# Packing the matmuls of a score bound into column strips and moving the work around them, in a segmented attention and GLU kernel

## The chip, the cores and the metric

The kernel runs on one core of one Trainium2 chip. The metric is the device time of one execution in microseconds (us), as median of several runs. All runs used below are of the fast state. The engines are PE (tensor engine), PEld (its weight loads), DVE (vector), ACT (scalar), POOL (GpSimd) and SP, whose queue (SPq) issues most of the DMA transfers.

## The reference

Input x has 2048 tokens of 640 features, in bf16. The sequence is cut into four segments of 512 tokens; there are 32 heads of 20 features.

```python
xn = layernorm(x)
q, k, v = xn @ wq, xn @ wk, xn @ wv
for s in range(4):                               # segments
    logits = qs @ ks.T * scale + causal_mask
    a_dot  = softmax(logits) @ vs
    a_mem  = (phi(qs) @ M) / (phi(qs) @ z + 1e-6)
    o      = g * a_mem + (1 - g) * a_dot
    M, z   = M + phi(ks).T @ vs, z + sum(phi(ks))
s   = o @ wo
glu = (sigmoid(xn @ w_gate) * (xn @ w_up)) @ w_down
out = x + s * silu(glu)
```

## The kernel before

Each segment has 20 slots. A slot computes scores of four heads (tile Sps), their exponentials on ACT (pt), the product of earlier exponentials with V (Aps), and takes further PE work from a plan (projections of the next segment, memory update) and from a queue of dense GLU matmuls. The program emits PE's instructions in the order of this plan, so the plan decides which work PE has next.

The softmax is kept in range by a bound on each score: for a head and a query, the sum over the 20 features of |q| times the largest |k| in the segment. It is a small matrix product, with minus the largest |k| as weights, nonzero only at the features of each head (tile ik), and |q| as moving operand (tile aq). The result goes as a 21st row next to the 20 rows of q, against a row of ones in k, so the score matmul subtracts it.

```python
def bound_mm(n, half):                       # twice per segment, 16 heads each
    ik, aq = seg[n]["ik"], seg[n]["aq"]
    cps = ps_d.tile([16, L], F32, name="cps", tag="d")
    for i in range(3):                       # three chunks of 128 features
        nc.tensor.matmul(cps[:], lhsT=ik[:, i, :], rhs=aq[:, i, :], start=(i == 0), stop=(i == 2))
    cb = stg.tile([16, L], BF, name="cb", bufs=2)
    nc.vector.tensor_copy(cb[:], cps[:])
    seg[n]["cb", half] = cb

def bound_dma(n, half, engs):                # SBUF to SBUF, one row per head
    cb = seg[n]["cb", half]
    for r in range(4):
        engs[r % len(engs)].dma_start(QT[32*r + DH:32*r + E1, 4*half:4*half + 4, :], cb[4*r:4*r + 4, :])

def scores(unit):                            # E1 = 21 rows
    ...
    nc.tensor.matmul(Sps[:, r, c0:c0 + ncol], lhsT=KT[32*r:32*r + E1, g, ...],
                     rhs=QT[32*r:32*r + E1, g, q0:L], ..., tile_position=(32*r, 0))

# plan of segment n for the next segment m (slot, work):
for slot, fn, c in [(9, do_K, 0), (10, do_K, 1), (11, do_K, 2), (11, do_Q, 0), (12, do_Q, 1), (13, do_Q, 2),
                    (14, do_Q, 3), (15, do_Q, 4), (16, do_K, 3), (17, do_K, 4)]: ...
for i in range(8): at(10 + i, V_NS, do_V, m, i // 2, i % 2, nc.scalar)
... at(13, 800, m_update, n, 0); at(14, 520, m_update, n, 1)
... at(15, C_NS, bound_mm, m, 0) ... at(19, C_NS, bound_mm, m, 1)

# first segment: three gate/up pairs run before the first scores
do_gate(0, 0); do_up(0, 0); bound_mm(0, 1); ...
for f in (1, 2): do_gate(0, f); do_up(0, f)
```

## Time and profile before

| | before |
|---|---|
| median, first four runs | 343.95 us (343.78 to 344.16) |
| span of the profiled run | 342.0 us |
| PE / DVE / ACT busy | 97% / 65% / 65% |
| share of PE in the chain of waits | 86% |
| bound matmuls | 24, in eight groups of three |

The page of the profiled execution of the kernel before, its first part (busy time of each engine, share of the span, instructions) and the head of its fourth (the chain of work that ended last, by engine):

```profile
span 342.0 us, 8153 instructions
PE 331.2 (97%) x3327; PEld 183.8 (54%) x3370; DVE 221.4 (65%) x516; ACT 221.8 (65%) x218; POOL 100.1 (29%) x172
...
PE 86%; DVE 5%; ACT 4%; issue 3%; POOL 1%; ACTq 0%; POOLq 0%
```

PE is the bottleneck. A matmul's busy time is modelled and overlaps with the next one (0.379 us is shown below where the next starts after 0.218 us), so for sizes it is better to look at when the next instruction starts. The view of the tile cps, and the timeline around one bound group (start us, duration us, engine, line, operation, count), kernel before:

```profile
L287 PE MATMUL cps<-aq,ik x24: 379/379/383, 23.4 to 253.2; 128*16 128x512 bf16 x24
L289 DVE CAST cb<-cps x8: 669/679/679, 25.1 to 253.6; 16x512 bf16<-16x512 f32 x8
```

```profile
91.69 0.81 PE L287 MATMUL cps<-aq,ik 128*16 128x512 bf16 x3
92.35 0.42 ACT L306 CAST V<-psv 128x320 bf16<-128x320 f32 x1
92.44 0.41 PE L467 MATMUL Sps<-QT,KT 21*128 21x384 bf16 x8
```

The three matmuls hold PE from 91.69 to 92.44 us, 0.75 us. In the recorded starts they are 0.218 us apart, and the next kind of matmul starts 0.311 us after the third. Eight groups make 6.0 us. The same timeline at the first scores of the program, and who PE waited for (total us, times, longest us):

```profile
27.95 2.58 SPq L295 DMA_DIRECT2D QT<-cb  x4
...
33.72 0.40 PE L467 MATMUL Sps<-QT,KT 21*128 21x512 bf16 x4
```

```profile
PE up L380 <- ACT tg L374: 0.9, 1, 0.9
PE psv L301 <- DVE ktd L244: 0.8, 1, 0.8
PE Sps L467 <- ACT pt L475: 0.5, 1, 0.5
```

The first scores start without a wait, and the named waits later on are few and below 1 us each.

### The profile page before, as it was taken

The numbers are of one execution on the slowest core, as the hardware profiler recorded it, in microseconds if no ns is written. First come the engines' busy times: TensorE is split into PE (matmuls) and PEld (weight loads), VectorE is DVE, ScalarE is ACT, GpSimd is POOL, SyncE is SP. The second block draws the span as 40 slices with busy tenths as digits, with TensorE's granted clock in tenths as the row PEclk, the third lists the DMA queues.
The fourth block names the chain that finished last, engine by engine and source line by source line (L and its number), as shares of the span: only waits on it lengthen the run. The fifth ranks groups of instructions, "written<-read, shape, count | busy, mean of one in ns | idle before, by whom it ended". The sixth has DMA issues, their size and how long they took to land.

```text
span 342.0 us, 8153 instructions
## 1 busy us (share of the span) xinstructions
PE 331.2 (97%) x3327; PEld 183.8 (54%) x3370; DVE 221.4 (65%) x516; ACT 221.8 (65%) x218; POOL 100.1 (29%) x172
## 2 busy tenths in 40 slices
PE   8999999999999999999999999999999999999995
PEld 3544444656544555556566455545446655544763
DVE  5374465475776776798768786878765575553355
ACT  2523777677786866766787657667965766767620
POOL 6800224223222243223232422222223223232122
PEclk9999999999999999999999999999999999999999
DMA  7987792302247614113365326014134000000132
GB/s 220 384 320 211 156 306 101 80 2 84 86 143 140 154 44 120 49 67 105 80 187 149 79 77 98 21 65 144 36 108 136 22 21 21 20 21 2 58 67 77
DMA packets 51574, 36.45 MB, mean 107 GB/s; under 512 B 27345, under 2 KB 50257, under 8 KB 51537
## 3 DMA queue, kind: packets, MB, share of 16 engines
q1 hardware_dynamic: 50224, 32.00, 33.7%
q10 hardware_dynamic: 1312, 3.93, 2.9%
q8 instruction: 26, 0.43, 0.5%
q14 instruction: 12, 0.09, 0.1%
HBM read 17.05 MB, written 12.32 MB: 86 GB/s over the span
## 4 chain that ended last, share of the span: by engine, by line
PE 86%; DVE 5%; ACT 4%; issue 3%; POOL 1%; ACTq 0%; POOLq 0%
PE yp L394 16%; PE up L380 14%; PE gp L371 13%; PE psq L239 11%; PE Aps L496 9%; PE Sps L467 7%; PE psv L301 6%; PE sp L418 4%; PE am L356 2%; PE cps L287 2%; ACT pt L475 1%; PE dm L337 1%; PE sp L448 1%; ACT mn L317 1%; ACT V L306 1%
## 5 line engine op out<-in xcount | busy, mean ns | idle before, releaser
L475 ACT ACTIVATE pt<-Sps 128x2048 bf16<-128x2048 f32 (+1 forms) x81 | 150.3, 1855 | 35.2 <-PE Sps L467 32.0
L477 POOL TENSOR_SCALAR_AFFINE_SELECT pt<-pt 128x512 bf16<-128x512 bf16 x128 | 80.7, 646 | 226.7 <-ACT pt L475 226.7
L380 PE MATMUL up<-xnT,Wu 128*128 128x512 bf16 x228 | 59.1, 379 | 1.7 <-ACT tg L374 0.9
L371 PE MATMUL gp<-xnT,Wg 128*128 128x512 bf16 x225 | 58.9, 379 | 1.0 <-ACT V L306 0.2
L394 PE MATMUL yp<-Wd,hT 128*128 128x320 bf16 x384 | 57.5, 299 | 0.0
L383 DVE SCALAR_TENSOR_TENSOR hT<-tg,up 128x512 bf16<-128x512 bf16 x48 | 32.8, 684 | 35.9 <-PE up L380 26.6
L496 PEld LDWEIGHTS <-pt 128*128 128x128 bf16 x1280 | 42.7, 96 | 14.4 <-issue 3.0
L374 ACT ACTIVATE tg<-gp 128x512 bf16<-128x512 f32 x48 | 28.5, 594 | 26.0 <-PE gp L371 26.0
L496 PE MATMUL Aps<-V,pt 128*128 128x21 bf16 x1280 | 44.6, 173 | 0.0
L394 PEld LDWEIGHTS <-hT 128*128 128x128 bf16 x384 | 35.3, 97 | 15.3 <-issue 2.6
L398 DVE SCALAR_TENSOR_TENSOR aa<-t,yp 128x320 bf16<-128x320 bf16 x32 | 15.6, 488 | 32.8 <-ACT t L397 32.7
L380 PEld LDWEIGHTS <-Wu 128*128 128x128 bf16 x240 | 21.1, 97 | 24.4 <-issue 4.3
L371 PEld LDWEIGHTS <-Wg 128*128 128x128 bf16 x240 | 21.4, 97 | 23.7 <-issue 3.2
L467 PE MATMUL Sps<-QT,KT 21*128 21x128 bf16 (+3 forms) x512 | 32.3, 301 | 0.5 <-ACT pt L475 0.5
L301 PE MATMUL psv<-Wv,xnT 128*128 128x320 bf16 x160 | 26.5, 299 | 1.1 <-DVE ktd L244 0.8
L397 ACT ACTIVATE t<-yp 128x320 bf16<-128x320 f32 x32 | 13.9, 435 | 20.0 <-PE yp L394 19.7
L239 PE MATMUL psq<-xnT,Wq 128*128 128x512 bf16 x93 | 24.0, 378 | 0.4
L239 PE MATMUL psq<-xnT,Wk 128*128 128x512 bf16 x91 | 23.7, 378 | 0.5
L467 PEld LDWEIGHTS <-KT 21*128 21x128 bf16 x512 | 9.5, 92 | 26.8 <-issue 26.3
L306 ACT CAST V<-psv 128x320 bf16<-128x320 f32 x32 | 13.7, 427 | 15.1 <-PE psv L301 14.7
L301 PEld LDWEIGHTS <-xnT 128*128 128x128 bf16 x160 | 15.4, 98 | 11.4 <-issue 1.1
L418 PE MATMUL sp<-Wo,oT 128*128 128x320 bf16 x120 | 20.2, 298 | 0.2 <-ACT tg L374 0.2
(77 smaller groups left out, 309.1 us busy)
## 6 DMA issues: line engine op xcount, KB each, us to landing
KT<-Kd SPq DMA_DIRECT2D x32, 80.0 KB
QT<-Qd SPq DMA_DIRECT2D x32, 80.0 KB
out_dram<-xt SPq DMA_DIRECT2D x15, 160.0 KB
Wg<-in_B_w_gate_dram ACTq DMA_DIRECT2D x1, 1920.0 KB
Wu<-in_B_w_up_dram ACTq DMA_DIRECT2D x1, 1920.0 KB
xt<-in_A_x_dram SPq DMA_DIRECT2D x3, 640.0 KB
Wd<-in_B_w_down_dram SPq DMA_DIRECT2D x1, 1920.0 KB
Xd<-xn SPq DMA_DIRECT2D x12, 160.0 KB
```

Of the source, the lines that this page charges most:

```text
L239: nc.tensor.matmul(ps[:], lhsT=W[:, k, c * P:(c + 1) * P], rhs=xnT_of[n][:, k, :], start=(k == 0), stop=(k == DC - 1))
L301: nc.tensor.matmul(ps[:], lhsT=xnT_of[n][:, k, j * P:(j + 1) * P], rhs=Wv[:, k, half * HD:(half + 1) * HD], start=(k == 0), stop=(k == DC ...
L371: nc.tensor.matmul(gp[:], lhsT=Wg[:, k, f * P:(f + 1) * P], rhs=xnT_of[n][:, k, :], start=(k == 0), stop=(k == DC - 1))
L374: nc.scalar.activation(tg[:], gp[:], ACT.Tanh, scale=0.5)
L380: nc.tensor.matmul(up[:], lhsT=Wu[:, k, f * P:(f + 1) * P], rhs=xnT_of[n][:, k, :], start=(k == 0), stop=(k == DC - 1))
L383: nc.vector.scalar_tensor_tensor(out=h[:], in0=seg[n]["tg"][:], scalar=1.0, in1=up[:], op0=ALU.add, op1=ALU.mult)
L394: nc.tensor.matmul(yp[:], lhsT=s["hT"][f][:, j * P:(j + 1) * P], rhs=Wd[:, f, hs], start=(f == 0), stop=(f == FC - 1))
L418: nc.tensor.matmul(sp[:], lhsT=s["oT"][:, c, j * P:(j + 1) * P], rhs=Wo[:, c, hs], start=(c == 0), stop=(c == DC - 1))
L467: nc.tensor.matmul(Sps[:, r, c0:c0 + ncol], lhsT=KT[32 * r:32 * r + E1, g, kb * P:(kb + 1) * P], rhs=QT[32 * r:32 * r + E1, g, q0:L], star ...
L475: nc.scalar.activation(pt[:, :, 0:ntot], Sps[:, :, 0:ntot], ACT.Exp, scale=SCALE)
L477: nc.gpsimd.affine_select(out=pt[:, :, c0:c0 + P], in_=pt[:, :, c0:c0 + P], compare_op=ALU.is_ge, fill=0.0, base=0, pattern=[[0, 4], [1, P ...
L496: nc.tensor.matmul(acc["ps"][:, qb, r, :], lhsT=t[:, r, off:off + P], rhs=V[n % 2][:, kb, 4 * g + r, :], start=acc["fresh"], stop=True, sk ...
```

## The change

Its intent is to make the bound cheaper on PE. One group of five matmuls per segment replaces two groups of three. The five go into three strips of 32 columns of the PE array, so that up to three run at once. The three partial sums are not added: they go to the scores as rows 21 to 23, and the score matmul adds them. The bound now passes through DRAM to reach its rows. Since one group needs all of Q and K, these projections are squeezed into slots 9 to 14, and V, phi and the memory update move later. The start is re-ordered too (blocks of x before weights, the first transpose in two parts, index masks built later), and a fourth gate/up pair runs before the first scores. In the excerpt, `...` marks cuts, and lines of the bound functions that only allocate or hand on tiles are left out.

```diff
+    Bd = [dpool.tile([3 * H, L], BF, name=f"Bd{i}") for i in range(2)]
 ...
-    def bound_mm(n, half):
-        cps = ps_d.tile([16, L], F32, name="cps", tag="d")
-        for i in range(3):
-            nc.tensor.matmul(cps[:], lhsT=ik[:, i, :], rhs=aq[:, i, :], start=(i == 0), stop=(i == 2))
+    def bound_mm(n):
+        cps = ps_d.tile([3 * H, L], F32, name="cps", tag="d")
+        for c in range(DC):                                   # DC = 5, H = 32
+            i = c % 3
+            nc.tensor.matmul(cps[H * i:H * i + H, :], lhsT=ik[:, c, :], rhs=aq[:, c, :],
+                             start=(c < 3), stop=(c >= 2), tile_position=(0, H * i), skip_group_check=True)
+        nc.vector.tensor_copy(cb[:], cps[:])
+        nc.sync.dma_start(Bd[n % 2][:], cb[:])
+    def bound_dma(n, half):
+        src = Bd[n % 2][:].rearrange("(i r g) n -> r i g n", i=3, r=4)
+        for r in range(4):
+            nc.sync.dma_start(QT[32*r + DH:32*r + DH + 3, 4*half:4*half + 4, :], src[r][:, 4*half:4*half + 4, :])
 ...
-                                 lhsT=KT[32 * r:32 * r + E1, g, ...
+                                 lhsT=KT[32 * r:32 * r + DH + 3, g, ...
 ...  (the start: cut)
-    for f in (1, 2):
+    for f in (1, 2, 3):
 ...
-(9, do_K, 0), (10, do_K, 1), (11, do_K, 2), (11, do_Q, 0), (12, do_Q, 1), (13, do_Q, 2), (14, do_Q, 3), (15, do_Q, 4), (16, do_K, 3), (17, do_K, 4)
+(9, do_K, 0), (10, do_K, 1), (10, do_K, 2), (11, do_Q, 0), (11, do_Q, 1), (12, do_Q, 2), (12, do_Q, 3), (13, do_Q, 4), (13, do_K, 3), (14, do_K, 4)
-            at(10 + i, V_NS, do_V, m, i // 2, i % 2, nc.scalar)
+            at(12 + i, V_NS, do_V, m, i // 2, i % 2, nc.scalar)
-        at(13, 800, m_update, n, 0)
+        at(17, 800, m_update, n, 0)
-        at(15, C_NS, bound_mm, m, 0)   ...   at(19, C_NS, bound_mm, m, 1)
+        at(16, C_NS, bound_mm, m)
```

More of the change, by code (lines that the diff above doesn't have):

```diff
@@ L134 @@
     beta_b = cpool.tile([P, H], BF, name="beta_b")
-    for half in range(2):
-        load_x(0, ((2 * half, 2 * half + 1), (2 * half + 1, 2 * half + 2)))
-        hs = slice(half * HD, (half + 1) * HD)
-        nc.sync.dma_start(Wv[:, :, hs], A_wv[:, hs].rearrange("(c p) n -> p c n", p=P))
+    for half, blocks in ((0, (0, 1)), (1, (2,)), (None, (3,))):
+        load_x(0, [(j, j + 1) for j in blocks])
+        if half is not None:
+            hs = slice(half * HD, (half + 1) * HD)
+            nc.sync.dma_start(Wv[:, :, hs], A_wv[:, hs].rearrange("(c p) n -> p c n", p=P))
     load_w(nc.sync, Wk, A_wk)
@@ L151 @@
     nc.gpsimd.memset(KT[:].bitcast(mybir.dt.uint32), 0x3F803F80)
-    Ind = []
-    for hb in range(2):
-        t = cpool.tile([P, 3, 4, 4], F32, name=f"Ind{hb}")
-        nc.gpsimd.memset(t[:], -1.0)
-        base = 2 * hb * P - 16 * hb * DH
-        nc.gpsimd.affine_select(out=t[:], in_=t[:], compare_op=ALU.is_ge, fill=0.0, base=base,
-                                pattern=[[P, 3], [-DH, 4], [-4 * DH, 4]], channel_multiplier=1)
-        nc.gpsimd.affine_select(out=t[:], in_=t[:], compare_op=ALU.is_ge, fill=0.0, base=DH - 1 - base,
-                                pattern=[[-P, 3], [DH, 4], [4 * DH, 4]], channel_multiplier=-1)
-        Ind.append(t)
+    Ind = cpool.tile([P, DC, 4, NG], F32, name="Ind")
     V = [cpool.tile([P, 4, H, E1], BF, name=f"V{i}") for i in range(2)]
@@ L167, in late_constants @@
         nc.gpsimd.tensor_copy(BD[:, 0:1], after[:, 0:1])
+        nc.gpsimd.memset(Ind[:], -1.0)
+        nc.gpsimd.affine_select(out=Ind[:], in_=Ind[:], compare_op=ALU.is_ge, fill=0.0, base=0,
+                                pattern=[[P, DC], [-DH, 4], [-4 * DH, NG]], channel_multiplier=1)
+        nc.gpsimd.affine_select(out=Ind[:], in_=Ind[:], compare_op=ALU.is_ge, fill=0.0, base=DH - 1,
+                                pattern=[[-P, DC], [DH, 4], [4 * DH, NG]], channel_multiplier=-1)
         for i in range(2):
@@ L267, in relayout @@
             eng.dma_start(dst[32 * r:32 * r + DH, 4 * half:4 * half + 4, :], src[r])
-    def bound_q(n, half):
-        aq = stg.tile([P, 3, L], BF, name="aq")
-        U16 = mybir.dt.uint16
-        nc.vector.tensor_scalar(aq[:].bitcast(U16), seg[n]["qt"][:, 2 * half:2 * half + 3, :].bitcast(U16),
-                                0x7FFF, None, op0=ALU.bitwise_and)
-        seg[n]["aq"] = aq
-    def bound_k(n, half):
-        ik = stg.tile([P, 3, 16], BF, name="ik", bufs=2)
-        nc.vector.tensor_tensor(
-            ik[:], Ind[half][:].rearrange("p c r g -> p c (r g)"),
-            seg[n]["kabs"][:, 2 * half:2 * half + 3].unsqueeze(2).to_broadcast([P, 3, 16]), op=ALU.mult)
-        seg[n]["ik"] = ik
@@ L283, in bound_mm, with bound @@
-    def bound_mm(n, half):
-        ik, aq = seg[n]["ik"], seg[n]["aq"]
-        cps = ps_d.tile([16, L], F32, name="cps", tag="d")
-        for i in range(3):
-            nc.tensor.matmul(cps[:], lhsT=ik[:, i, :], rhs=aq[:, i, :], start=(i == 0), stop=(i == 2))
-        cb = stg.tile([16, L], BF, name="cb", bufs=2)
+    def bound(n):
+        s = seg[n]
+        ik = stg.tile([P, DC, H], BF, name="ik")
+        nc.vector.tensor_tensor(ik[:], Ind[:].rearrange("p c r g -> p c (r g)"),
+                                s["kabs"][:].unsqueeze(2).to_broadcast([P, DC, H]), op=ALU.mult)
+        aq = stg.tile([P, DC, L], BF, name="aq")
+        U16 = mybir.dt.uint16
+        nc.vector.tensor_scalar(aq[:].bitcast(U16), s["qt"][:].bitcast(U16), 0x7FFF, None, op0=ALU.bitwise_and)
+        s["bound"] = ik, aq
@@ L289, in bound_mm @@
+    def bound_mm(n):
+        ik, aq = seg[n]["bound"]
+        cps = ps_d.tile([3 * H, L], F32, name="cps", tag="d")
[3 more added lines that the diff above has]
+                             start=(c < 3), stop=(c >= 2), tile_position=(0, H * i), skip_group_check=True)
+        cb = stg.tile([3 * H, L], BF, name="cb")
         nc.vector.tensor_copy(cb[:], cps[:])
-        seg[n]["cb", half] = cb
-    def bound_dma(n, half, engs):
-        cb = seg[n]["cb", half]
+        nc.sync.dma_start(Bd[n % 2][:], cb[:])
@@ L294, in bound_dma @@
+    def bound_dma(n, half):
+        src = Bd[n % 2][:].rearrange("(i r g) n -> r i g n", i=3, r=4)
         for r in range(4):
-            engs[r % len(engs)].dma_start(QT[32 * r + DH:32 * r + E1, 4 * half:4 * half + 4, :],
-                                          cb[4 * r:4 * r + 4, :])
+            nc.sync.dma_start(QT[32 * r + DH:32 * r + DH + 3, 4 * half:4 * half + 4, :],
+                              src[r][:, 4 * half:4 * half + 4, :])
     def do_V(n, j, half, evac):
@@ L467, in scores @@
                 nc.tensor.matmul(Sps[:, r, c0:c0 + ncol],
-                                 lhsT=KT[32 * r:32 * r + E1, g, kb * P:(kb + 1) * P],
-                                 rhs=QT[32 * r:32 * r + E1, g, q0:L],
+                                 lhsT=KT[32 * r:32 * r + DH + 3, g, kb * P:(kb + 1) * P],
+                                 rhs=QT[32 * r:32 * r + DH + 3, g, q0:L],
                                  start=True, stop=True, tile_position=(32 * r, 0))
@@ L535, with stats0, first_transpose, norm0 @@
     xns = {}
-    def ln0(j):
-        xns[j] = ln_norm(0, j, mv, rs)
-    for pair in range(2):
-        for j in (2 * pair, 2 * pair + 1):
-            ln_stats(0, j, mv)
-            ln_rstd(mv, rs, slice(j, j + 1))
-        for j in (2 * pair, 2 * pair + 1):
-            ln0(j)
-    late_constants(xns[3])
-    for j in range(4):
-        ln_transpose(0, j, xns[j], nc.scalar)
-        if j < 2:
-            w, src = ((Wg, B_w_gate), (Wu, B_w_up))[j]
-            load_w(nc.scalar, w, src)
-        if j == 0:
-            keep_warm(3)
-        if j == 1:
-            do_V(0, 0, 0, nc.scalar)
-            do_V(0, 1, 0, nc.scalar)
-        if j == 2:
-            do_V(0, 0, 1, nc.scalar)
-            do_V(0, 1, 1, nc.scalar)
-            do_V(0, 2, 0, nc.scalar)
+    def stats0(j):
+        ln_stats(0, j, mv)
+        ln_rstd(mv, rs, slice(j, j + 1))
+    def first_transpose():
+        xnT_of[0] = xpool.tile([P, DC, L], BF, name="xnT")
+        for c0, c1 in ((0, 3), (3, 5)):
+            pT = ps_d.tile([P, c1 - c0, P], BF, name="pT", tag="d")
+            for c in range(c0, c1):
+                nc.tensor.transpose(pT[:, c - c0, :], xns[0][:, c * P:(c + 1) * P], ident[:])
+            dst = xnT_of[0][:, c0:c1, 0:P]
+            if c0:
+                nc.vector.tensor_copy(dst, pT[:])
+            else:
+                nc.scalar.copy(dst, pT[:])
+    def norm0(j):
+        xns[j] = ln_norm(0, j, mv, rs)
+    stats0(0)
+    stats0(1)
+    norm0(0)
+    first_transpose()
+    load_w(nc.scalar, Wg, B_w_gate)
+    stats0(2)
+    norm0(1)
+    keep_warm(2)
+    do_V(0, 0, 0, nc.scalar)
+    ln_transpose(0, 1, xns[1], nc.scalar)
+    load_w(nc.scalar, Wu, B_w_up)
+    norm0(2)
+    stats0(3)
+    do_V(0, 0, 1, nc.scalar)
+    do_V(0, 1, 0, nc.scalar)
+    ln_transpose(0, 2, xns[2], nc.scalar)
+    norm0(3)
+    late_constants(xns[3])
+    do_V(0, 1, 1, nc.scalar)
+    do_V(0, 2, 0, nc.scalar)
+    ln_transpose(0, 3, xns[3], nc.scalar)
     do_V(0, 2, 1, nc.scalar)
-    for half in range(2):
-        do_V(0, 3, half, nc.scalar)
-    for c in range(3):
+    do_V(0, 3, 0, nc.scalar)
+    do_V(0, 3, 1, nc.scalar)
+    for c in range(5):
         do_K(0, c, nc.vector)
-    spill(0, 0, nc.sync, None)
+        if c == 2:
+            spill(0, 0, nc.sync, None)
     for c in range(3):
@@ L571 @@
     relayout(0, 0, Qd, QT, nc.sync)
-    load_x(1)
-    bound_k(0, 0)
-    bound_q(0, 0)
-    do_K(0, 3, nc.vector)
-    do_K(0, 4, nc.vector)
-    bound_mm(0, 0)
-    bound_dma(0, 0, [nc.sync])
     for c in range(3, 5):
         do_Q(0, c, nc.scalar)
-    spill(0, 1, nc.sync, nc.sync)
-    bound_k(0, 1)
-    bound_q(0, 1)
-    k_tok(0)
+    bound(0)
     do_gate(0, 0)
     do_up(0, 0)
-    bound_mm(0, 1)
+    bound_mm(0)
+    bound_dma(0, 0)
+    load_x(1)
+    spill(0, 1, nc.sync, nc.sync)
+    k_tok(0)
     relayout(0, 1, Kd, KT, nc.sync)
     relayout(0, 1, Qd, QT, nc.sync)
-    bound_dma(0, 1, [nc.sync])
+    bound_dma(0, 1)
     gates()
@@ L598 @@
     GLU_NS, V_NS, TR_NS, DN_NS = DC * mm_ns(L), DC * mm_ns(HD), DC * mm_ns(P), FC * mm_ns(HD)
-    MEM_NS, C_NS = 220, 3 * mm_ns(L)
+    MEM_NS, C_NS = 220, 2 * mm_ns(L) + 200
     def segment_plan(n):
@@ L632, in segment_plan @@
         at(9, 0, new_seg, m)
-        for slot, fn, c in [(9, do_K, 0), (10, do_K, 1), (11, do_K, 2), (11, do_Q, 0), (12, do_Q, 1), (13, do_Q, 2),
-                            (14, do_Q, 3), (15, do_Q, 4), (16, do_K, 3), (17, do_K, 4)]:
+        for slot, fn, c in [(9, do_K, 0), (10, do_K, 1), (10, do_K, 2), (11, do_Q, 0), (11, do_Q, 1), (12, do_Q, 2),
+                            (12, do_Q, 3), (13, do_Q, 4), (13, do_K, 3), (14, do_K, 4)]:
             at(slot, GLU_NS, fn, m, c, nc.vector)
         for i in range(8):
-            at(10 + i, V_NS, do_V, m, i // 2, i % 2, nc.scalar)
-        for part in range(2):
-            at(9 + 2 * part, 0, phi, n, "ktok", "phik", 2 * part, 2 * part + 2)
-            at(10 + 2 * part, 0, phi_end, n, "phik", 2 * part)
-        at(13, 800, m_update, n, 0)
-        at(14, 520, m_update, n, 1)
-        at(12, 0, spill, m, 0, nc.sync, None)
-        at(13, 0, relayout, m, 0, Kd, KT, nc.sync)
-        at(14, 0, spill, m, 0, None, nc.sync)
-        at(14, 0, bound_k, m, 0)
-        at(14, 0, bound_q, m, 0)
-        at(15, C_NS, bound_mm, m, 0)
-        at(15, 0, relayout, m, 0, Qd, QT, nc.sync)
-        at(15, 0, phi, m, "qt", "phiq", 0, 2)
-        at(16, 0, phi_end, m, "phiq", 0)
-        at(16, 0, bound_dma, m, 0, [nc.sync])
-        at(16, 0, spill, m, 1, None, nc.sync)
-        at(16, 0, bound_q, m, 1)
+            at(12 + i, V_NS, do_V, m, i // 2, i % 2, nc.scalar)
+        at(11, 0, spill, m, 0, nc.sync, None)
+        at(12, 0, relayout, m, 0, Kd, KT, nc.sync)
+        at(13, 0, spill, m, 0, None, nc.sync)
+        at(14, 0, relayout, m, 0, Qd, QT, nc.sync)
+        at(14, 0, spill, m, 1, None, nc.sync)
+        at(15, 0, bound, m)
+        at(15, 0, spill, m, 1, nc.sync, None)
+        at(16, C_NS, bound_mm, m)
+        at(16, 0, phi, m, "qt", "phiq", 0, 2)
+        at(17, 0, phi_end, m, "phiq", 0)
+        at(17, 0, bound_dma, m, 0)
         at(17, 0, phi, m, "qt", "phiq", 2, 5)
         at(18, 0, phi_end, m, "phiq", 2)
-        at(18, 0, spill, m, 1, nc.sync, None)
-        at(18, 0, bound_k, m, 1)
-        at(19, C_NS, bound_mm, m, 1)
+        for part in range(2):
+            at(12 + 2 * part, 0, phi, n, "ktok", "phik", 2 * part, 2 * part + 2)
+            at(13 + 2 * part, 0, phi_end, n, "phik", 2 * part)
+        at(17, 800, m_update, n, 0)
+        at(18, 520, m_update, n, 1)
         if m < NSEG - 1:
@@ L676 @@
     for n in range(NSEG):
-        for f in range(3 if n == 0 else 0, FC):
+        for f in range(4 if n == 0 else 0, FC):
             dense.append((n, GLU_NS, lambda n=n, f=f: do_gate(n, f)))
@@ L735 @@
             relayout(n + 1, 1, Qd, QT, nc.sync)
-            bound_dma(n + 1, 1, [nc.sync])
+            bound_dma(n + 1, 1)
     fill(1e12)
```

## The prediction

> **What bounds the kernel now.** The tensor engine (PE). The page gives PE 97% of the 342.0 us span (DVE 65%, ACT 65%, POOL 29%), and the chain of waits puts 86% of the span on PE. Modelled busy time overlaps, so I also read matmul starts: from 7 to 337.7 us they follow each other (0.216 us per 512-column, 0.136 us per 320-column matmul). Single waits over 0.25 us after 14 us add up to only about 3.5 us; the largest at 101.8 (0.64), 223.4 (0.96, for DVE to empty a PSUM buffer) and 247.3 us (1.06). Only less PE work, or those waits, can pay.
>
> **What the change removes.** The bound matmuls run eight times as three serial matmuls. Starts show 0.218 us twice, then 0.311 us until the next kind starts: 0.75 us a group, 6.0 us in all. The change runs four groups of five, packed three abreast in 32-column strips. The Trainium skill ("TensorE: Matmul & The Clock Gate", Part 3, measured speedup) gives 2.38x for three such column tiles; this case's trace shows packing by rows: the four score matmuls of 512 columns start 3 ns apart and hold PE 0.33 us together. Estimate from these: 0.22 + 0.33 = 0.55 us a group, 2.2 us in all. Saved: 3.8 us, all critical; without overlap about 1.3 us.
>
> DVE: four fewer PSUM copies of 0.68 us, four fewer small multiplies of 0.2 us, less masking: about 4 us of 221, off the critical path except at those waits. Scores of 23 rows should cost what 21 rows did. One warm-up matmul (0.22 us) goes. POOL's index masks leave the start, so the first reciprocal root (now 4.85 us) starts 0.6 us sooner; warm-up matmuls until 5.9 us hide half.
>
> **What it adds and moves.** (1) The bound goes through DRAM: a write, then reads. Spill to re-read takes 2.5 to 3 us in the queue's waits. Segment 0's bound also waits for all five Q blocks. Estimate: copy done 29.5, write landed 32.4, reads landed about 36. PE, with four gate/up pairs instead of three, reaches the first scores near 35. New wait: about 1 us (0 to 2). Later segments: none. (2) At the start the second transpose comes about 1 us later than now (8.6 instead of 7.4 us): 0 to 0.5 us lost before the K projections (now 14.5 us). (3) K and Q of the next segment are squeezed into six slots; DVE needs about 4 us there per slot of 3.3 us, but phi and the memory update move later. Waits for PSUM may shrink or grow: -0.7 us, give or take 1.5.
>
> **Sum.** 343.95 - 3.8 - 0.2 + 0.3 + 1.0 - 0.7 = 340.5 us; range 338.2 to 343.2. Chances: faster by over 2% 0.07, within 2% 0.91, slower 0.02.
>
> **What would show it.** Bound (cps) groups: starts of three abreast within 10 ns, group about 0.55 us. First scores at 34.5 to 36.5 us (now 33.7), with a wait for the QT transfer before. K projections starting at 14.3 to 15. PE still 96 to 97%, with waits of ktd/qtd evictions on DVE in slots 10 to 14 of segments 1 and 2.
>
> **What would make it wrong.** Strips that run serially (342 to 343 us); DVE falling behind in the squeezed slots by over 1 us per segment; a QT transfer late by several us; or the moved memory update removing all the waits (337.5 us).

## The result

The changed kernel takes 340.1 us (median of 10 runs, 339.73 to 341.21); the kernel before, in the same rounds, 344.14 us. The ratio is 0.9879, with a 95% interval of 0.9864 to 0.9894. By the record's limit of 2% this counts as "same", but the interval excludes no change. Ratios and intervals here and below are taken over the fast runs of both kernels in the same rounds, so they are not quite the ratio of the medians. An unedited repeat later, beside the last experiments, gave 340.18 us and 0.9885:

> The changed kernel itself, unedited, in the same rounds as the runs above, so that they can be compared with it on one chip: 340.1 us, a ratio of 0.988 to the kernel before.

The page of the changed kernel, the same lines as before:

```profile
span 337.8 us, 8139 instructions
PE 326.5 (97%) x3323; PEld 182.5 (54%) x3365; DVE 217.8 (64%) x505; ACT 219.9 (65%) x218; POOL 99.9 (30%) x169
...
PE 83%; ACT 7%; DVE 5%; issue 2%; DMA 1%; SPq 1%; ACTq 0%
```

PE is still at 97%, but ACT has a larger share of the chain. The tile cps and the timeline of the bound group and the first scores in the first segment, changed kernel:

```profile
L281 PE MATMUL cps<-aq,ik x20: 379/389/390, 27.6 to 239.2; 128*32 128x512 bf16 x20
L284 DVE CAST cb<-cps x4: 675/680/686, 28.4 to 239.7; 96x512 bf16<-96x512 f32 x4
```

```profile
27.65 0.61 PE L281 MATMUL cps<-aq,ik 128*32 128x512 bf16 x5
28.19 1.25 PE L366 MATMUL gp<-xnT,Wg 128*128 128x512 bf16 x5
28.44 0.68 DVE L284 CAST cb<-cps 96x512 bf16<-96x512 f32 x1
29.15 0.32 SPq L285 DMA_DIRECT2D Bd<-cb  x1
...
31.72 1.18 SPq L290 DMA_DIRECT2D QT<-Bd  x4
...
34.77 0.39 PE L462 MATMUL Sps<-QT,KT 23*128 23x512 bf16 x4
```

Five matmuls hold PE from 27.65 to 28.19 us, 0.54 us, where three held it 0.75 us. Matmuls of different strips start 4 ns apart. The first scores start at 34.77 us and are not marked as having waited. Who PE waited for in the changed kernel (the first line is the wait at the very start, which the kernel before has too):

```profile
PE wps L525 <- DVE mn L134: 1.2, 1, 1.2
PE Sps L462 <- ACT pt L470: 1.0, 1, 1.0
PE up L375 <- ACT tg L369: 0.6, 1, 0.6
```

The wait for DVE to empty a projection buffer is gone from the head of the list, and new waits for ACT stand there.

To see where 4 us went I added up, from the recorded starts of all matmuls, the time that each kind holds PE beyond its own pace (pace: the median from one start to the next, such as 0.216 us for 512 columns; records that are missing are counted in). This splits the time to the last matmul (us):

```
                       bound   excess beyond pace           last
                       groups  before K  K..scores  later   matmul
before                  5.97     3.83      0.29     11.11   337.67
changed                 2.16     3.99      0.18     11.21   333.79
  the same, repeated    2.16     4.30      0.18     11.19   334.08   (c_after)
changed, bound serial   4.60     4.31      0.08     10.05   335.30   (e1_serial)
before, bound via DRAM  6.08     3.42      0.08     11.56   337.60   (e2c_nopack)
  and packed            3.46     3.38      0.29     13.04   336.64   (e2b_packonly)
```

The repeat shows how far one trace can be trusted: the columns after the first K projection agree within 0.02 us, and the start differs by 0.31 us. The first record of full clock comes at 4.36 us in one and at 7.02 us in the other (7.17 us in the kernel before).

From before to changed the last matmul comes 3.88 us earlier. The bound groups give 3.81 us of it and the warm-up matmul that was dropped 0.22 us; the excess is the same in sum. So far the result looks like the main term of the prediction and nothing else. The experiments show that this is too simple.

### The profile page after: what moved, and what is told of

Read it like the earlier page. It is cut to its first block, busy times and chain, and to the rows that moved or that the text cites. A ratio compares the mean times of both kernels' runs of the same rounds, so it can differ in the third digit from the quotient of the medians.

```text
span 337.8 us, 8139 instructions
## 1 busy us (share of the span) xinstructions
PE 326.5 (97%) x3323; PEld 182.5 (54%) x3365; DVE 217.8 (64%) x505; ACT 219.9 (65%) x218; POOL 99.9 (30%) x169
## 4 chain that ended last, share of the span: by engine, by line
PE 83%; ACT 7%; DVE 5%; issue 2%; DMA 1%; SPq 1%; ACTq 0%
PE gp L366 15%; PE up L375 14%; PE yp L389 14%; PE psq L236 11%; PE Aps L491 8%; PE Sps L462 7%; PE sp L413 5%; PE psv L296 4%; ACT pt L470 3%; PE am L351 2%; ACT mn L312 2%; DMA xt<-in_A_x_dram 1%; PE sp L443 1%; PE dm L332 1%; ACT V L301 1%
## 5 line engine op out<-in xcount | busy, mean ns | idle before, releaser
L393 DVE SCALAR_TENSOR_TENSOR aa<-t,yp 128x320 bf16<-128x320 bf16 x32 | 15.5, 486 | 31.9 <-ACT t L392 31.7
L375 PEld LDWEIGHTS <-Wu 128*128 128x128 bf16 x240 | 21.8, 97 | 23.2 <-issue 2.8
L462 PE MATMUL Sps<-QT,KT 23*128 23x128 bf16 (+3 forms) x512 | 32.4, 301 | 1.6 <-ACT pt L470 1.0
L462 PEld LDWEIGHTS <-KT 23*128 23x128 bf16 x512 | 9.8, 92 | 27.5 <-issue 26.5
L236 PE MATMUL psq<-xnT,Wq 128*128 128x512 bf16 x95 | 22.8, 378 | 0.3
L236 PE MATMUL psq<-xnT,Wk 128*128 128x512 bf16 x92 | 22.8, 378 | 0.3
L296 PEld LDWEIGHTS <-xnT 128*128 128x128 bf16 x160 | 14.0, 97 | 7.8 <-ACT xnT L216 1.4
```

The lines of the kernel that those rows point to most:

```text
L236: nc.tensor.matmul(ps[:], lhsT=W[:, k, c * P:(c + 1) * P], rhs=xnT_of[n][:, k, :], start=(k == 0), stop=(k == DC - 1))
L296: nc.tensor.matmul(ps[:], lhsT=xnT_of[n][:, k, j * P:(j + 1) * P], rhs=Wv[:, k, half * HD:(half + 1) * HD], start=(k == 0), stop=(k == DC ...
L375: nc.tensor.matmul(up[:], lhsT=Wu[:, k, f * P:(f + 1) * P], rhs=xnT_of[n][:, k, :], start=(k == 0), stop=(k == DC - 1))
L462: nc.tensor.matmul(Sps[:, r, c0:c0 + ncol], lhsT=KT[32 * r:32 * r + DH + 3, g, kb * P:(kb + 1) * P], rhs=QT[32 * r:32 * r + DH + 3, g, q0: ...
```

## The experiments

Theory: the gain is the PE time of the bound groups, which is on the critical path. Rival: it comes from the new order of work and from fewer DVE copies, and packing does little. All outputs are right. Ratios are to the kernel before in the same rounds.

### Packing taken out of the changed kernel (e1_serial)

```diff
-        ik = stg.tile([P, DC, H], BF, name="ik")              # in bound(n)
+        ik = ikz                                              # zeroed once; two DVE multiplies fill the strips, not one
 ...
-            nc.tensor.matmul(cps[H * i:H * i + H, :], lhsT=ik[:, c, :], rhs=aq[:, c, :],
-                             start=(c < 3), stop=(c >= 2), tile_position=(0, H * i), skip_group_check=True)
+            nc.tensor.matmul(cps[:], lhsT=ik[:, 3 * c:3 * c + 3, :].rearrange("p i h -> p (i h)"), rhs=aq[:, c, :],
+                             start=(c == 0), stop=(c == DC - 1))      # 96 columns, zeros outside strip c % 3
```

> The changed kernel with its five bound matmuls of a segment made serial again: weights of 96 columns with zeros outside the strip, so that all five accumulate one after the other and give the same three partial sums. Nothing else moves. Packing theory (the gain is the PE time of the bound groups): a group goes from 0.53 us to 4 x 0.218 + 0.311 = 1.18 us, four groups, so the run takes 2.6 us longer than the changed kernel, about 342.7 us. Rival theory (the gain comes from the new order of work and the fewer DVE copies): no more than 0.5 us longer, about 340.3 us.

Measured: 341.1 us, ratio 0.9907 (0.9890 to 0.9925). Three groups take 1.18 us each, as expected, and the first 1.08 us, yet the run is only 1.0 us longer than the changed kernel (from different rounds; the two intervals together leave about 0.2 to 1.8 us), less than half of the 2.6 us that the theory wanted and more than the 0.5 us of the rival. The table shows why: the bound takes 2.44 us more, but the later excess is 1.16 us less. The timelines show the clearest place, in the third segment. First the changed kernel, then the one with the serial bound:

```profile
238.96 1.06 ACT L312 ACTIVATE mn<-mn 128x1024 bf16<-128x1024 bf16 x1 [0.17 <-DVE mn L311]
238.99 0.61 PE L281 MATMUL cps<-aq,ik 128*32 128x512 bf16 x5
239.53 0.41 PE L462 MATMUL Sps<-QT,KT 23*128 23x256 bf16 x8
...
239.93 0.58 ACT L369 ACTIVATE tg<-gp 128x512 bf16<-128x512 f32 x1
...
240.56 1.24 PE L375 MATMUL up<-xnT,Wu 128*128 128x512 bf16 x4 [0.62 <-ACT tg L369]
```

```profile
240.44 1.24 PE L285 MATMUL cps<-aq,ikz 128*96 128x512 bf16 x5
240.50 1.06 ACT L316 ACTIVATE mn<-mn 128x1024 bf16<-128x1024 bf16 x1 [0.16 <-DVE mn L315]
241.46 0.58 ACT L373 ACTIVATE tg<-gp 128x512 bf16<-128x512 f32 x1
241.61 0.41 PE L466 MATMUL Sps<-QT,KT 23*128 23x256 bf16 x8
...
242.09 1.24 PE L379 MATMUL up<-xnT,Wu 128*128 128x512 bf16 x4
```

In both, ACT needs from about the start of the bound until 1.5 to 1.6 us later for two activations (mn and tg), and the up projection cannot start before. With the short group PE is done early and stands 0.62 us. With the long group the up projection starts without any wait. Here the whole saving of packing is paid back within a microsecond. Comparing the starts of each slot's scores in the two traces, each of the three later groups costs the serial kernel 0.53 to 0.54 us at first; 0.19, 0.08 and 0.55 us come back after the groups of the first, second and third segment's plan, 0.82 us in all. The remaining 0.32 us of the difference in the table lies at the start, where the PE clock was released at 4.4 us in one run and 7.3 us in the other; the repeat of the changed kernel, released at 7.0 us, has the same 4.3 us there, so this is scatter.

So not all of the 1.16 us is waiting. In the changed kernel the last matmul before each bound group holds PE 0.093 us longer than its pace, where PE goes from the whole array to strips of it (the last one of a V projection takes 0.229 us from start to start in place of 0.136 us); before the 96-column groups of e1_serial it is not (0.136 us). The packed groups pay this change of tile shape, and the table counts it as excess: 0.28 us in the later column, 0.37 us for all four groups. Packing thus saves 2.44 - 0.37 = 2.07 us of PE time here, and 0.82 us of it comes back as waits.

### Packing alone in the kernel before (e2_packonly, e2b_packonly, e2c_nopack)

```diff
-        for i in range(3):
-            nc.tensor.matmul(cps[:], lhsT=ik[:, i, :], rhs=aq[:, i, :], start=(i == 0), stop=(i == 2))
+        for i in range(3):                                    # still two groups of three per segment
+            nc.tensor.matmul(cps[H * i:H * i + H, :], lhsT=ik[:, i, :], rhs=aq[:, i, :],
+                             start=True, stop=True, tile_position=(0, H * i), skip_group_check=True)
+        nc.sync.dma_start(Bd[2 * (n % 2) + half][:], cb[:])   # then four reads into QT rows 21 to 23
```

One index mask of all heads replaces the two of the kernel before, in the same place.

> The kernel before, with its order of work, its eight half groups and its eight DVE copies, and only the packing taken over: the three matmuls of a half go into three strips of 32 columns, and the bound goes through DRAM as three rows. Packing theory: a group goes from 0.75 to 0.32 us, eight groups, so 3.4 us shorter than the kernel before, about 340.7 us, if the first scores do not wait for the bound; up to 1 us more if they do. Rival theory (order of work and fewer copies make the gain): about 344 us.

Measured: 347.63 us, ratio 1.0091 (1.0066 to 1.0116). It is slower than the kernel before, although its groups take 0.33 us instead of 0.75. The timeline at the first scores and PE's longest wait say why:

```profile
28.75 0.40 SPq L120 DMA_DIRECT2D xt<-in_A_x_dram  x1
...
29.25 0.45 SPq L287 DMA_DIRECT2D Bd<-cb  x1
...
34.78 1.18 SPq L292 DMA_DIRECT2D QT<-Bd  x4
...
36.59 1.56 PE L464 MATMUL Sps<-QT,KT 23*128 23x512 bf16 x4 [3.80 <-DMA QT<-Bd]
38.08 2.31 PE L368 MATMUL gp<-xnT,Wg 128*128 128x512 bf16 x5
```

The write of the bound queued behind the load of the next 640 KB of x. The reads could be issued only 5.5 us after the write (2.6 us in the changed kernel, 3.4 us in the mended run below), and PE stood 3.8 us. Then five gate matmuls took 2.31 us where they take 1.25 us otherwise: the trace records a granted clock of one half from 35.7 us for 6.83 us. The wait itself was paid, and then paid again. All four runs have a mean clock of 0.990 to 0.994, so each will have had such a stretch.

The run was mended by moving the load of x behind the reads and by running four gate/up pairs first:

```diff
-    load_x(1)                       # before the bound
+    load_x(1)                       # after bound_dma(0, 0)
-    for f in (1, 2):
+    for f in (1, 2, 3):
```

> The packing alone in the kernel before, as in the run before, but with the late bound taken out of it: in that run the write of the bound queued behind the load of the next 640 KB of x and PE waited 3.96 us for the first scores and then ran 6.8 us at half clock. Now the load of x comes after the reads of the bound, and four gate/up pairs cover the way through DRAM. Packing theory: the eight groups take 2.7 instead of 6.0 us and nothing else is lost, about 340.9 us. Rival (the new order of work in the later segments makes the gain): about 344 us. If the first scores still wait over 1 us and the clock drops: 343 us or more.

Measured: 342.59 us, ratio 0.9937 (0.9909 to 0.9966). It gains about 2.2 us, not 3.2. The counterpart has the same way through DRAM but serial matmuls (96 columns with zeros, as above):

> The run of the packing alone (kernel before, bound through DRAM, four gate/up pairs, load of x late) with the packing taken out again: weights of 96 columns with zeros outside the strip, three serial matmuls a half, same result. It splits the 2.2 us that this step gained, where the bound groups alone had gone from 5.97 to about 2.7 us. If the way through DRAM and the later load cost about 1 us: this run about 1 us above the kernel before, and packing is worth its 3.2 us. If the way through DRAM is free and new waits swallow part of the packing's gain: this run equals the kernel before within 0.3 us, and packing is worth about 2 us in the old order.

Measured: 343.49 us, ratio 0.9984 (0.9965 to 1.0003), the same as the kernel before. So the way through DRAM costs nothing once it is covered, and packing in the old order is worth the difference of these two: 0.9 us by the medians, 0.96 us by the last matmul, 1.6 us by the ratios. The two runs come from different rounds, in which the median of the kernel before differs by 1.1 us, so the ratios compare better than the medians; their intervals leave 1.6 us with some 1.2 us either way. The groups alone had promised 2.9 us (without waits the eight serial groups, 0.65 to 0.74 us each, take 5.5 us, the packed ones 2.6 us). Changes of tile shape before the eight packed groups, which the 96-column groups do not have, take 0.70 us of this, and most of the rest is again in new waits; the longest waits in the packed version are on ACT and DVE (the serial version has 1.7 and 1.0 us in the same two places):

```profile
PE up L377 <- ACT tg L371: 2.1, 4, 0.9
PE Aps L493 <- DVE od L518: 1.5, 2, 0.9
```

In its row of the table the later excess rises by 1.48 us against the serial counterpart, 0.51 us of it for the tile shape and 0.97 us in waits. In both rows two groups are followed by a wait that the table counts to the groups, 0.57 us in the serial and 0.84 us in the packed version. So about 1.2 us of waits are new.

### The bound taken away (e3_nobound)

```diff
     def bound_mm(n):
+        return
     def bound_dma(n, half):
+        return
-    lhsT=KT[32 * r:32 * r + DH + 3, ...
+    lhsT=KT[32 * r:32 * r + DH, ...
```

> The changed kernel without the bound's matmuls, their copies and their transfers; the scores use the 20 rows of data alone (the bound only keeps the exponential in range, and with these inputs it is not needed, so the output should still agree). The DVE preparation of the bound stays. Packing theory: what is left of the bound on PE is 2.1 us, so about 338.0 us. Rival (its DVE copies and transfers matter as well): below 337.5 us. If the bound were hidden now: about 340 us.

Measured: 337.48 us, ratio 0.9807 (0.9788 to 0.9826), 2.6 us below the changed kernel. In the trace the groups gave 2.16 us and the excess fell by 0.5 us, 0.37 us of that because no tile shape changes before a group. Here nothing came back as waits: what is left of the bound counts in full. The time is at the edge between the two expectations, so it does not separate them well. What is left of the bound costs 2 to 3 us. It is not a version to ship: the bound protects the exponential for other inputs.

### Three gate/up pairs in place of four (e4_threepairs)

```diff
-    for f in (1, 2, 3):
+    for f in (1, 2):
```

> The changed kernel with three gate/up pairs before the first scores, as the kernel before had, in place of four; the fourth moves behind. PE then reaches the first scores at about 32.6 us, while the last read of the bound is issued at 32.9 us. If the bound's way through DRAM is what the fourth pair covers, the first scores wait until the read lands, 33.5 to 34.7 us, and the run takes 0.9 to 2.1 us longer than the changed kernel, about 341.5 us. If the fourth pair covers nothing: 340.1 us.

Measured: 344.32 us, ratio 0.9996 (0.9967 to 1.0025): leaving out this one pair before the first scores undoes the whole change.

```profile
31.94 1.18 SPq L290 DMA_DIRECT2D QT<-Bd  x4
...
33.74 1.33 PE L462 MATMUL Sps<-QT,KT 23*128 23x512 bf16 x4 [1.11 <-DMA QT<-Bd]
...
35.01 2.11 PE L366 MATMUL gp<-xnT,Wg 128*128 128x512 bf16 x5
36.91 1.49 PE L375 MATMUL up<-xnT,Wu 128*128 128x512 bf16 x3
```

PE waits for the first of the four reads, and then the four score matmuls, which otherwise start within 10 ns, start at 33.74, 34.07, 34.24 and 34.70 us, one as each read lands. So the last read lands at about 34.7 us here; in the changed kernel, whose reads are issued 0.2 us sooner, PE comes for it at 34.77 us. The fourth pair covers the way through DRAM with a few tenths of a microsecond to spare. The expectation had the wait right (about 2.1 us in all) but not what follows it: the clock falls to one half for 3.41 us from 35.25 us on, and some later waits grow as well (the later excess is 15.1 us against 11.2; of these 3.9 us, 0.9 are the wait between the score matmuls and 1.7 the half clock).

Only the profiled run has a trace, and the clock did not fall in all of them: the mean clock is 0.994 and 0.993 in the runs of 344.87 and 344.80 us, but 0.999 in those of 343.83 and 342.95 us, which are still 2.9 to 3.7 us above the changed kernel. So the wait and what follows it costs this much without the half clock. The slowest run of the changed kernel itself, 341.21 us, has a mean clock of 0.995, about what 3.4 us at half clock would leave of 339 us (an estimate; it has no trace). The margin of the fourth pair may not always hold.

### The old slots with one late group (e6_oldslots)

```diff
-(9, do_K, 0), (10, do_K, 1), (10, do_K, 2), (11, do_Q, 0), ... (13, do_K, 3), (14, do_K, 4)
+(9, do_K, 0), (10, do_K, 1), (11, do_K, 2), (11, do_Q, 0), ... (16, do_K, 3), (17, do_K, 4)
-        at(16, C_NS, bound_mm, m)     # and V, phi, m_update in the new slots
+        at(19, C_NS, bound_mm_dma, m) # and V, phi, m_update in the old slots
```

> The changed kernel with the old slots for K, Q, V, phi and the memory update; the one bound group, which needs all of K and Q, then comes in the last slot of a segment in place of slot 16. Theory (the squeeze is there so that the one group and its way through DRAM are done before the next segment's first scores): PE waits 2.5 to 4 us at each of the three segment borders and may fall to half clock after each, 350 to 360 us. Rival (the squeeze does nothing for the bound, only for the waits inside a segment): 340 to 341 us.

Measured: 358.77 us, ratio 1.0424 (1.0393 to 1.0456). PE waits at all three segment borders, 11.8 us in all (totals, times and longest), and the clock falls to one half for 6.83 us after each:

```profile
PE Sps L471 <- DMA QT<-Bd: 7.5, 2, 4.5
PE Sps L471 <- DMA KT<-Kd: 4.3, 1, 4.3
```

So the new slots are what a single group with its way through DRAM needs; they do not have to earn anything by themselves. The edit moves V, phi and the memory update back as well, so it does not show that the squeeze of K and Q alone is needed.

### The start (e5_oldstart, e7_start) and the last K projections (e8_spread, e10_both)

The old start put back into the changed kernel (loads, statistics, transposes, V and warm-up matmuls as before):

> The changed kernel with the start of the kernel before (order of loads, statistics, transposes, V, three warm-up matmuls) up to the first K projection; the late index masks stay. The prediction held that the new start loses 0 to 0.5 us, so the old one should be up to 0.3 us faster net of the warm-up matmul. The traces put the first K projection at 14.66 us before and 14.60 us after. Start theory: within 0.3 us of the changed kernel, 339.8 to 340.4 us. Rival (the new start is part of the gain): 341 us or more.

Measured: 339.68 us, ratio 0.9855 (0.9831 to 0.9879). The new start gives no part of the gain; it may cost some 0.4 us, but the intervals overlap.

A start with the second normalisation and the statistics of blocks 2 and 3 earlier:

```diff
-    stats0(2); norm0(1); keep_warm(2); do_V(0, 0, 0, ...); ln_transpose(0, 1, ...); norm0(2); stats0(3)
+    norm0(1); stats0(2); stats0(3); keep_warm(2); do_V(0, 0, 0, ...); ln_transpose(0, 1, ...); norm0(2); norm0(3)
-    ln_transpose(0, 3, xns[3], nc.scalar)
+    ln_transpose(0, 3, xns[3], nc.vector)
```

> The changed kernel with a start that keeps DVE ahead of PE: the second normalisation and the statistics of blocks 2 and 3 come earlier, and the last transpose is evicted by DVE. In the trace PE waits 0.7 us before the second transpose and 0.3 us three times for the eviction of a transpose. If these waits are worth their length: first K projection at about 13.7 us in place of 14.6 and 339.3 us. If DVE or the loads of x hold it as before: 340.1 us.

Measured: 339.85 us, ratio 0.9864 (0.9832 to 0.9896). The first K projection comes at 13.98 us in place of 14.60 (14.92 in the repeat), so the waits were real, but the time is within its own scatter of 339.24 to 341.05 us.

The last two K projections one slot later each:

```diff
-(13, do_Q, 4), (13, do_K, 3), (14, do_K, 4)   # bound in slot 15
+(13, do_Q, 4), (14, do_K, 3), (15, do_K, 4)   # bound in slot 16
```

> The changed kernel with the last two K projections of the next segment one slot later each (slots 14 and 15 in place of 13 and 14, the bound's preparation in 16). The change's squeeze leaves slot 15 with so little PE work that PE waits 1.15 us at 163 us for the exponentials. If the squeeze made that wait: it goes, about 339.2 us. If the wait only moves: 340.1 us.

Measured: 339.69 us, ratio 0.9854 (0.9825 to 0.9883). The wait of 1.15 us at 163 us for the exponentials is gone, but PE now waits 0.6 us at 168.8 us for ACT and 0.4 us before a bound group for DVE, the up projection's wait for ACT at 240.6 us grew from 0.6 to 0.8 us, and the later excess is 11.01 us against 11.21: the wait mostly moved.

Both edits together:

> The changed kernel with the new start and the spread K projections together, the two edits that measured 339.85 and 339.69 us alone. If both gains are real and add: 339.2 us or less. If one or both were noise of 0.1%: 339.6 to 340.0 us.

Measured: 339.41 us, ratio 0.9862 (0.9837 to 0.9888). It has the lowest median of all that keep the bound, but the two intervals overlap, so that it beats the changed kernel is likely and not shown.

## Why the prediction was right

The measured 340.1 us lies in the range, 0.4 us from the predicted 340.5. Point by point:

- **PE bounds the kernel.** Right: 97% busy before and after.
- **The packed groups.** Right in size: 0.54 us a group against 0.55 predicted, strips 4 ns apart, 3.81 us less group time against 3.8. The Trainium skill ("TensorE: Matmul & The Clock Gate", Part 3, measured speedup) gives 2.38x for three column tiles; here three matmuls fell from 0.75 to 0.33 us, 2.3x, close to it.
- **"Saved: 3.8 us, all critical."** For the change as a whole the sum came out, but this does not hold for the packing by itself. Taking packing out of the changed kernel returned 2.44 us of group time, 2.07 us net of the tile shape, but cost only 1.0 us; putting it alone into the old order removed 2.9 us of group time, 2.2 us net, and paid 0.9 to 1.6 us. PE work is exchanged with waits for ACT and DVE: when a group gets shorter, PE arrives sooner at a result that is no sooner there. It is no rule, since e3_nobound got the remaining group time in full.
- **What paid the rest.** Everything except packing (e1_serial) already gains about 3.2 us by its ratio. Its trace shows 2.4 us: 1.37 us from the groups (20 serial matmuls for 24), 0.70 us because 96-column groups have no change of tile shape before them (the eight 16-column groups of the kernel before have one, 0.08 to 0.09 us each), 0.22 us from the warm-up matmul and 0.55 us from fewer later waits, less 0.48 us at the start. Then packing takes 2.07 us off, net of the tile shape, and 0.82 us of waits come back. The two movements of the waits nearly cancel: between the kernel before and the changed one, later waits proper rise by 0.33 us, and four changes of tile shape fewer take the same 0.33 us off, which nobody predicted. Which of the moved pieces or spared DVE copies lowered the waits was not separated and stays open.
- **"-0.7 us" for the waits on PSUM.** The later excess changed by +0.10 us (waits alone +0.33 us), so this term had the wrong sign. The forecast waits of projection evictions on DVE in slots 10 to 14 did not come to the head; the largest new wait is for ACT's exponentials.
- **"New wait: about 1 us" at the first scores.** It was zero. The write was read back after 2.6 us, within the 2.5 to 3 us assumed, but the mis-sized term is the reads: 3.6 us had been put between the landed write and the landed reads (32.4 to 36 us), and about 2.8 us were needed (31.7 to about 34.5 us; the end is inferred from e4_threepairs, where it shows). The margin is small.
- **"+0.3 us" at the start.** The trace shows +0.16 us of excess before the first K projection, which comes at 14.60 us in place of 14.66; e5_oldstart would fit about 0.4 us. The trace of the changed kernel happens to have an early clock (4.36 us). The repeat, whose clock is as late as that of the kernel before (7.02 and 7.17 us), has its first K projection at 14.92 us and +0.47 us of excess, so the forecast loss at the start was about right.

The three small terms summed to +0.6 us, and what the traces show for them is +0.15 us, or +0.44 us in the repeat (the three columns of excess). That they came so close is luck: the wait of 1.0 us that did not come and the 0.7 us of waits that did not go have opposite signs. The total was right because the large term was right as net sum, not because every line of it was.

## What to carry to other kernels

Saved time on the busiest engine is worth its full length only where no other engine's result is due right after it; look at the next instruction after the shortened group and at what it waits for, and reckon with a part of the gain coming back as waits even at 97% busy. Test the packing apart from the re-ordering, in both orders of work, before crediting either. When a cheaper computation takes a slower path to its user, put enough independent PE work in front of the first use, because a PE wait can be charged a second time by a half-speed clock: by the mean clocks, 2.1 us of waiting were in two of four runs of e4_threepairs, and 3.8 us in all four of e2_packonly.

## What the Trainium skill lacked or had wrong

- "TensorE: Matmul & The Clock Gate" (Why this matters for your kernels) advises against PE-idle gaps over about 3 us. Here about 2.1 us of waiting, in several parts within 2.5 us, could be enough: the clock fell to one half for 3.41 us in the profiled run of e4_threepairs, and by the mean clocks in two of its four runs. A wait of 3.8 us was followed by 6.83 us at half clock in all (e2_packonly). These lengths fit one and two of the 3.4 us windows that the page describes (Part 1, What's actually happening).
- "TensorEngine Tiling (Array Packing)" (Key Properties) says that a change of tiling mode drains the engine, without a size. Here the last matmul of a bound group held PE 0.31 us, where one of 512 columns followed by its own kind holds it 0.216 us, and the V projection before a bound group 0.229 in place of 0.136 us. That is about 0.1 us a change, for the narrow unpacked group of the kernel before as well. The 96-column group of e1_serial that is followed by a gate matmul pays nothing (0.216 us).
- "DMA: Bandwidth & Descriptors" (Anatomy of one DMA, SWDGE path) fits about 2.0 us plus the bytes for one DMA of the software path, and gives no such time for a write from SP's queue that is read back, alone or behind other transfers of its queue. Here 96 KB could be read back 2.6 us after the issue of the write in the first segment and 1.7 us after it in the second (changed kernel), and 5.5 us after it when 640 KB of another load were queued ahead (e2_packonly).
